# A matrix-memory attention and an expert layer on one core: the hand-written order of 1595 operations replaced by another

## Chip, cores and metric

One core of one Trainium2 chip. The time is device microseconds of one launch of the whole kernel; the number that counts is the median of several runs.

## What is computed

For 4 batches, 8 heads and 768 steps with head size 40, a recurrence with gates (an mLSTM), followed by one expert layer over the 3072 tokens. Cut to what matters:

```python
for t in range(S):
    m_new = np.maximum(f_gate[:, :, t] + m, i_gate[:, :, t])
    f_stab, i_stab = np.exp(f_gate[:, :, t] + m - m_new), np.exp(i_gate[:, :, t] - m_new)
    C = f_stab * C + i_stab * np.einsum('bhd,bhe->bhde', vt, kt)
    n = f_stab * n + i_stab * kt
    y[:, :, t] = sigmoid(o_gate[:, :, t]) * (C @ qt) / max(abs(n @ qt), 1)
...
x = y as (3072 tokens, 320)
h = x @ w_in                                  # 320 -> 2048
g = h * erf(softplus(h))
return g @ w_out                              # 2048 -> 320
```

## The kernel before

The 768 steps are cut into 12 chunks of 64; a chunk of all four batches is 256 tokens. `attention(c)` does a chunk in two halves of two batches each. For each half: scores of k and q on TensorE (PE, L507), times a decay matrix that VectorE applies (DVE, L562), then one accumulation on PE of the carried state (L516), the state's update (L521) and the values under the scores (L530), and on DVE the division, the output gate and the new state (L589 to L616). The half's result is transposed on PE (L389 to L393) and split by ScalarE and VectorE into a high and a low fp32r part, `xh` and `xl` (L402, L406). `gate_block(c)` makes the decays of two chunks at a time: a scan and some ten small operations on DVE, an exponential on ScalarE (ACT), and a round trip through a DRAM scratch `gd` that spreads one row over many partitions (L379, L456, L473).

`mlp(g)` is a quarter of the expert layer for one chunk (48 in all): the up product on PE (L748, two or four operations of 8 to 16 matmuls), copies out of PSUM on ACT (L759) and additions on DVE (L764), softplus and erf on ACT (L768, L772), the product on DVE (L776), a split into high and low fp32r parts `gh` and `gl` (L786 or L788, L792), and the down product on PE (L814 to L817; plain fp32 for the first four, L812). Exp, softplus and erf stand in three different activation tables; each change of table is one ACT_TABLE_LOAD (L876).

The weights arrive as 64-bit numbers. `decode` (L619) rebuilds a float in three operations, two on DVE (L624, L635) and one on ACT (L630); `halves` and `weights_tail` then split it in two (L645 and L649, L683 and L687). All of this happens once, beside the first chunks of attention.

Nothing is scheduled by a compiler. Every operation is recorded by `Plan.add` and has a number; `ORDER` (L94 to L166) lists the 1595 numbers in the order in which they are issued. Each engine works its own instructions off strictly in that order, and SyncE (SP) issues all DMAs in it, on one queue. A negative entry -n issues n warming matmuls at that place (`stay`, L867): matmuls on constants that keep TensorE's clock up and whose results nobody reads. Operation 11 (L279) is five more of them. When an operation needs another activation table than the one loaded, the load goes in just ahead of it (L81), so the number of loads follows from the order.

Names in this text: a00, a01, a10, a11 are the halves of chunks 0 and 1 (chunk, then half; the second half of a chunk comes first in the order); m0, m2, m4 are the first quarters of the expert layer for chunk 0, m47 the last one.

Of the kernel before, what the change touches and what calls it, by code (L numbers as in the profile page):

```python
# [33 lines left out]
class Plan:  # L34
# [60 lines left out]
    1, 4, 0, 3, 5, 7, 9, 11, 12, 6, 13, 2, 14, 15, 16, 8, 17, 33, 27, 32, 34, 36, 35, 20, 19, 31, 38, -1, 40, 28, 26, 29, 93,  # L95
    95, 349, 350, 351, 42, -2, 47, 94, 48, 49, 18, 67, 68, 99, 96, 10, 50, 59, 60, 25, 37, 30, 39, 52, 65, 23, 100, 101, 102,
    105, 107, 106, 108, 41, -2, 55, 44, 66, 72, 56, 109, 43, 24, 71, 354, 45, 46, 111, 112, 57, 74, 76, 58, 22, 69, 73, -1, 64,
    75, 70, 103, 104, 352, 353, 357, 97, 98, 51, 53, 135, 136, 137, 138, 63, 139, 110, 54, 140, 129, 130, 131, 132, 21, 169,
    171, 170, 133, 172, 61, 163, 358, 78, 83, 134, 86, 164, 84, 85, 221, 222, 165, 166, 62, 241, 157, 173, 174, 167, 168, 159,
    239, 240, 125, 127, 158, 160, 175, 199, 200, 161, 242, 88, 193, 77, 91, 201, 195, 205, 207, 223, 224, 225, 162, 273, 79,  # L100
    80, 81, 82, 87, 89, 274, 202, 203, 355, 371, 206, 141, 194, 142, 121, 92, 122, 275, 276, 90, 248, 226, 489, 208, 490, 491,
    204, 196, 249, 227, 356, 369, 113, 209, 250, 143, 197, 251, 361, 114, 372, 210, 115, 494, 149, 126, 128, 492, 457, 467,
    374, 198, 286, 287, 150, 123, 288, 373, 376, 230, 362, 363, 289, 176, 299, 493, 151, 231, 458, 459, 462, 124, 152, 495,
    117, 211, 116, 300, 118, 375, 119, 290, 252, 232, 243, 244, 380, 316, 317, 333, 120, 228, 366, 468, 370, 377, 291, 719,
    720, 378, 382, 212, 359, 364, 365, 721, 185, 384, 360, 496, 253, 145, 379, 392, 337, 233, 245, 389, 186, 724, 466, 368,
    146, 381, 177, 178, 153, 318, 154, 189, 229, 383, 190, 390, 391, 456, 394, 144, 301, 469, 472, 367, 191, 155, 147, 148,
    156, 246, 187, 385, 386, 387, 388, 460, 292, 498, 192, 397, 398, 188, 267, 319, 347, 217, 455, 218, 234, 343, 725, 393,
    395, 396, 268, 461, 474, 320, 277, 302, 235, 247, 181, 497, 399, 400, 278, 464, 475, 473, 236, 477, 465, 470, 334, 182,
    471, 981, 425, 479, 481, 482, 426, 213, 484, 321, 322, 219, 293, 261, 501, 401, 179, 605, 726, 511, 294, 254, 502, 402,
    427, 428, 183, 214, 595, 728, 303, 429, 215, 512, 265, 476, 438, 439, 478, 220, 412, 279, 184, 180, 266, 323, 259, 463,  # L110
    257, 335, 503, 271, 263, 280, 480, 488, 510, 485, 593, 509, 606, 258, 486, 237, 238, 216, 260, 324, 729, 264, 336, 487,
    499, 722, 504, 727, 262, 483, 338, 596, 272, 255, 256, 297, 430, 723, 513, 269, 270, 281, 516, 345, 304, 982, 305, 983,
    505, 295, 298, 500, 296, 325, 339, 340, 326, 327, 597, 440, 506, 431, 508, 986, 413, 306, 307, 329, 330, 414, 331, 519,
    284, 432, 403, 328, 514, 741, 525, 527, 532, 529, 282, 283, 530, 521, 522, 594, 515, 308, 309, 518, 285, 520, 441, 442,
    415, 416, 417, 418, 443, 341, 1243, 603, 523, 344, 524, 742, 312, 313, 310, 404, 405, 348, 526, 550, 551, 406, 576, 990,
    311, 528, 577, 314, 537, 538, 419, 598, 315, 407, 517, 507, 563, 564, 408, 731, 433, 533, 444, 536, 342, 1244, 531, 599,
    608, 740, 552, 553, 554, 607, 539, 540, 565, 732, 534, 535, 1245, 600, 602, 743, 746, 613, 615, 578, 420, 409, 619, 621,
    410, 411, 346, 421, 730, 604, 609, 626, 610, 623, 624, 601, 616, 612, 423, 541, 542, 445, 625, 543, 555, 566, 857, 858,
    859, 614, 617, 618, 611, 620, 424, 436, 579, 631, 632, 633, 640, 641, 642, 733, 736, 622, 634, 635, 630, 636, 652, 653,
    654, 984, 985, 1248, 673, 674, 675, 655, 748, 422, 656, 657, 734, 735, 446, 661, 662, 663, 739, 862, 679, 680, 681, 627,  # L120
    628, 434, 694, 695, 738, 696, 332, 1249, 867, 682, 683, 684, 437, 556, 637, 638, 639, 697, 698, 567, 749, 751, 699, 544,
    700, 701, 755, 658, 659, 660, 580, 664, 702, 545, 629, 451, 452, 453, 744, 745, 987, 703, 676, 435, 677, 678, 685, 752,
    757, 759, 762, 760, 643, 686, 447, 548, 549, 448, 557, 449, 750, 753, 754, 704, 705, 756, 546, 547, 788, 568, 569, 581,
    789, 790, 558, 570, 791, 792, 793, 559, 737, 761, 830, 831, 665, 832, 582, 836, 837, 838, 758, 571, 855, 839, 840, 841,
    687, 561, 809, 815, 562, 574, 988, 989, 810, 816, 811, 644, 450, 767, 868, 869, 872, 768, 817, 860, 861, 856, 766, 666,
    797, 747, 798, 560, 572, 769, 1246, 818, 819, 645, 646, 573, 763, 866, 874, 799, 864, 820, 1247, 764, 765, 873, 776, 777,
    778, 1003, 770, 771, 772, 647, 875, 583, 881, 1004, 1005, 584, 870, 1002, 1119, 575, 794, 795, 773, 774, 796, 775, 667,
    706, 877, 589, 833, 812, 590, 993, 994, 688, 834, 591, 454, 585, 586, 883, 587, 800, 835, 842, 813, 865, 650, 651, 671,
    888, 707, 843, 885, 886, 878, 814, 588, 648, 871, 1129, 1130, 863, 876, 879, 1120, 880, 649, 669, 991, 821, 914, 668, 670,
    690, 779, 689, 915, 916, 882, 708, 1131, 1134, 917, 918, 919, 935, 936, 937, 801, 672, 893, 894, 895, 709, 691, 938, 939,  # L130
    710, 940, 692, 693, 992, 592, 941, 715, 716, 780, 781, 802, 884, 956, 822, 995, 1008, 942, 943, 1010, 962, 887, 892, 957,
    958, 711, 782, 963, 964, 823, 920, 921, 922, 902, 903, 717, 1121, 712, 904, 889, 944, 945, 783, 946, 899, 786, 996, 997,
    900, 901, 1006, 713, 998, 824, 1000, 890, 1001, 896, 1250, 1255, 897, 898, 844, 803, 923, 924, 925, 947, 926, 804, 1128,
    1251, 1011, 825, 1017, 1256, 1007, 965, 966, 959, 960, 961, 891, 784, 1019, 1024, 1021, 1257, 1013, 905, 787, 785, 807,
    808, 1260, 805, 967, 968, 1014, 1022, 948, 1012, 999, 1015, 1016, 828, 1009, 927, 906, 806, 949, 1092, 1093, 1094, 1029,
    845, 829, 1030, 1031, 928, 1095, 1096, 1097, 826, 1018, 950, 951, 1050, 1098, 1020, 1051, 1099, 1052, 1100, 846, 714, 1252,
    1122, 907, 1035, 1036, 1037, 1025, 1026, 1028, 1038, 1039, 1135, 969, 1040, 1118, 1127, 1136, 1117, 1123, 851, 718, 1264,
    1265, 1056, 1124, 1126, 1381, 1057, 1058, 827, 847, 1053, 1054, 1055, 848, 849, 1059, 1060, 1061, 1023, 1101, 1102, 1103,
    929, 852, 970, 1382, 1032, 1125, 1071, 853, 1072, 1073, 1137, 930, 1143, 908, 1033, 1034, 1077, 909, 971, 1078, 1079, 1062,
    1063, 910, 1080, 1139, 1074, 1081, 912, 1027, 1145, 1253, 1147, 1150, 1148, 1140, 1075, 1076, 913, 1132, 1133, 1082, 1268,  # L140
    1254, 933, 934, 911, 954, 1138, 1104, 1105, 1106, 1141, 1142, 1064, 1083, 1041, 1144, 854, 972, 955, 977, 1262, 1149, 1176,
    1177, 1042, 1178, 931, 932, 1218, 1146, 1151, 1219, 1220, 1084, 978, 979, 1263, 980, 1224, 1225, 1226, 1043, 1155, 1156,
    952, 1197, 1157, 1065, 1198, 1152, 1199, 1044, 953, 1185, 1186, 1164, 1154, 1187, 1266, 1267, 1270, 1165, 1166, 973, 1383,
    1045, 974, 975, 1107, 1221, 1222, 1258, 1223, 1161, 1162, 1271, 1048, 1259, 1163, 1390, 1391, 1085, 1269, 1182, 1183, 1200,
    1201, 1184, 1202, 1066, 1153, 1273, 1158, 1159, 1160, 1227, 1228, 1229, 1049, 1275, 1276, 1179, 1180, 1086, 1279, 1181,
    1392, 1395, 1206, 1108, 1069, 1389, 976, 1203, 1167, 1207, 1204, 1070, 1379, 1281, 1286, 1283, 1188, 1189, 1046, 1047,
    1067, 1090, 1208, 1205, 1284, 1272, 1274, 1277, 1068, 1088, 1393, 1380, 1278, 1333, 1334, 1354, 1355, 1087, 1089, 1335,
    1280, 1357, 1358, 1261, 1387, 1356, 1359, 1291, 1292, 1293, 1282, 1287, 1288, 1388, 1360, 1361, 1168, 1362, 1290, 1339,
# [789 lines left out]
```

## Time and profile before

| what | us |
|---|---|
| median of 3 runs | 459.34 |
| lowest and highest run | 458.18, 461.6 |
| span of the profiled execution, first to last instruction | 456.7 |
| TensorE busy in that span | 445.6 (98%) |
| VectorE busy | 336.5 (74%) |
| ScalarE busy | 328.5 (72%) |
| GpSimd busy | 37.3 (8%) |

For the profiled execution the page gives the span alone; what lies around it is the launch and the end of the program, 1.5 us between its span and the lowest run, 2.6 us to the median. How to read it: the busy times say which engine is full on the average, but the first 40 us, the long middle and the last few us have different limits and are read apart. TensorE's busy time includes the warming matmuls.

### The profile page before, as it was taken

The numbers are of one execution on the slowest core, as the hardware profiler recorded it, in microseconds if no ns is written. First come the engines' busy times: TensorE is split into PE (matmuls) and PEld (weight loads), VectorE is DVE, ScalarE is ACT, GpSimd is POOL, SyncE is SP. The second block draws the span as 40 slices with busy tenths as digits, with TensorE's granted clock in tenths as the row PEclk, the third lists the DMA queues.
The fourth block names the chain that finished last, engine by engine and source line by source line (L and its number), as shares of the span: only waits on it lengthen the run. The fifth ranks groups of instructions, "written<-read, shape, count | busy, mean of one in ns | idle before, by whom it ended". The sixth has DMA issues, their size and how long they took to land.

```text
span 456.7 us, 14133 instructions
## 1 busy us (share of the span) xinstructions
PE 445.6 (98%) x6118; PEld 401.6 (88%) x6118; DVE 336.5 (74%) x657; ACT 328.5 (72%) x524; POOL 37.3 (8%) x62
## 2 busy tenths in 40 slices
PE   6979999999999999999999999999999999999996
PEld 4569988888999988989998998899898899999996
DVE  5899989799768766588468948776845869548762
ACT  4758999898976946855996984998445584773760
POOL 2000131003300220001021100001110000000000
PEclk9989999999999999999999999999999999999999
DMA  7889696836613430065405217342341100100011
GB/s 273 273 264 332 170 321 177 217 95 199 184 40 106 136 107 3 3 195 130 133 1 163 72 27 238 72 113 78 107 128 26 30 1 2 29 2 15 1 45 29
DMA packets 46831, 51.82 MB, mean 113 GB/s; under 512 B 27056, under 2 KB 31664, under 8 KB 46768
## 3 DMA queue, kind: packets, MB, share of 16 engines
q1 hardware_dynamic: 46768, 50.91, 38.2%
q8 instruction: 48, 0.79, 0.7%
q14 instruction: 15, 0.12, 0.1%
HBM read 46.77 MB, written 4.13 MB: 111 GB/s over the span
## 4 chain that ended last, share of the span: by engine, by line
PE 92%; DVE 3%; ACT 2%; DMA 1%; issue 1%; SPq 0%; DVEq 0%
PE h L748 40%; PE pob L816 11%; PE pob L814 11%; PE pob L817 11%; PE pa L530 3%; PE pa L507 3%; PE pa L516 3%; PE pa L812 2%; PE pob L812 2%; PE pa L521 2%; PE pa L389 2%; PE pa L444 1%; PE pob L873 1%; DMA eT<-gd 1%; DMA gt<-in_gates_dram 1%
## 5 line engine op out<-in xcount | busy, mean ns | idle before, releaser
L748 PE MATMUL h<-xh,wh 128*128 128x256 f32 (+1 forms) x768 | 201.4, 345 | 0.2 <-DVE hb L764 0.2
L748 PEld LDWEIGHTS h<-xh,wh 128*128 128x128 f32 x768 | 126.0, 190 | 14.1 <-DVE hb L764 0.5
L759 ACT ACTIVATE hb<-h 128x256 f32<-128x256 f32 (+1 forms) x160 | 66.7, 422 | 82.7 <-PE h L748 82.6
L748 PE MATMUL h<-xh,wl 128*128 128x256 f32 x384 | 108.5, 283 | 0.2 <-DVE wl L649 0.2
L816 PE MATMUL pob<-woh,gh 128*128 128x320 f32 x336 | 101.1, 313 | 0.0
L817 PE MATMUL pob<-wo,gh 128*128 128x320 f32 x336 | 100.1, 310 | 0.0
L764 DVE TENSOR_TENSOR hb<-h,hb 128x256 f32<-128x256 f32 x128 | 53.1, 420 | 45.8 <-ACT hb L759 45.2
L748 PEld LDWEIGHTS h<-xh,wl 128*128 128x128 f32 x384 | 72.9, 190 | 2.7 <-DVE wl L649 0.5
L876 ACT ACT_TABLE_LOAD x54 | 69.3, 1283 | 1.7 <-PEq L926 0.8
L776 DVE TENSOR_TENSOR n<-n,hb 128x1024 f32<-128x1024 f32 x48 | 58.6, 1227 | 14.8 <-ACT n L772 14.7
L817 PEld LDWEIGHTS pob<-wo,gh 128*128 128x128 f32 x336 | 63.2, 188 | 1.4
L816 PEld LDWEIGHTS pob<-woh,gh 128*128 128x128 f32 x336 | 63.2, 188 | 0.5
L814 PE MATMUL pob<-woh,gl 128*128 128x320 f32 x336 | 62.7, 312 | 0.0
L485 POOL TENSOR_SCALAR_AFFINE_SELECT dm<-dm 128x512 f32<-128x512 f32 (+1 forms) x40 | 34.0, 856 | 293.9 <-ACT dm L465 256.6
L792 DVE TENSOR_TENSOR gl<-n,gh 128x1024 fp32r<-128x1024 f32 x44 | 53.9, 1228 | 2.2 <-ACT gh L786 1.9
L814 PEld LDWEIGHTS pob<-woh,gl 128*128 128x128 f32 x336 | 53.5, 188 | 2.0
L768 ACT ACTIVATE n<-hb 128x1024 f32<-128x1024 f32 x48 | 49.3, 1058 | 1.6 <-DVE hb L764 1.3
L772 ACT ACTIVATE n<-n 128x1024 f32<-128x1024 f32 x48 | 49.6, 1054 | 0.2
L786 ACT ACTIVATE gh<-n 128x1024 fp32r<-128x1024 f32 x28 | 29.5, 1052 | 0.0
L406 DVE TENSOR_TENSOR xh<-pa,xh 128x384 fp32r<-128x384 f32 x24 | 13.3, 554 | 15.1 <-ACT xh L402 15.1
L562 DVE TENSOR_TENSOR dm<-pa,dm 128x512 f32<-128x512 f32 x24 | 16.5, 687 | 9.6 <-ACT xh L402 6.0
L530 PEld LDWEIGHTS pa<-kvo,dm 64*32 64x32 f32 x1536 | 16.7, 106 | 5.9 <-issue 5.0
(99 smaller groups left out, 469.6 us busy)
## 6 DMA issues: line engine op xcount, KB each, us to landing
qk<-in_qk_dram SPq DMA_DIRECT2D x24, 512.0 KB
kvo<-in_kvo_dram SPq DMA_DIRECT2D x24, 484.0 KB
eT<-gd SPq DMA_DIRECT2D x44, 128.0 KB
raw<-in_w_out_dram SPq DMA_DIRECT2D x16, 320.0 KB
dm<-gd SPq DMA_DIRECT2D x40, 128.0 KB
raw<-in_w_in_dram SPq DMA_DIRECT2D x8, 512.0 KB
out_dram<-o SPq DMA_DIRECT2D x48, 80.0 KB
raw<-in_w_in_dram SPq DMA_DIRECT2D x4, 256.0 KB
```

The source lines that it names most:

```text
L485: nc.gpsimd.affine_select(out=x, in_=x, pattern=[[0, H], [1, L]], compare_op=ALU.is_ge, fill=0.0, base=base, channel_multiplier=-1)
L748: nc.tensor.matmul(h[:, n * T:n * T + n_], w, m, start=(s == 0), stop=(s == len(ops) - 1))
L759: nc.scalar.activation(part(), G(f'h{i}')[:, T:2 * T] if wide else G(f'h{i}'), AF.Copy)
L764: nc.vector.tensor_tensor(part(), G(f'h{i}')[:, 0:T], part(), op=ALU.add)
L768: nc.scalar.activation(new('n0', [128, 1024], ('n0', g)), G('hb'), AF.Softplus)
L772: nc.scalar.activation(G('n0'), G('n0'), AF.Erf)
L776: nc.vector.tensor_tensor(G('n0'), G('n0'), G('hb'), op=ALU.mult)
L792: nc.vector.tensor_tensor(new('gl', [128, 1024], ('gl', g), F32R), G('n0'), G('gh').bitcast(F32), op=ALU.subtract)
L814: nc.tensor.matmul(acc(b), G('gl')[:, ts], woh[:, j], start=False, stop=(j == NFF - 1))
L816: nc.tensor.matmul(acc(b), G('gh')[:, ts], woh[:, j], start=(j == 0), stop=False)
L817: nc.tensor.matmul(acc(b), G('gh')[:, ts], t['wol', j], start=False, stop=False)
L876: plan.run(ORDER, lambda k: nc.scalar.preload_act_table_set(KIND[k]), stay)
```

## The change

`ORDER` is another permutation of the same 1595 operations with the same four warming entries (6 matmuls in all) at other places. No operation, tile, buffer count or DMA is changed. The table has one line more, so all later lines of the changed file are one higher (L748 becomes L749). Of the diff two lines are enough, since its numbers tell a reader nothing:

```diff
 ORDER = [
-    1, 4, 0, 3, 5, 7, 9, 11, 12, 6, 13, 2, 14, 15, 16, 8, 17, 33, 27, 32, 34, 36, 35, 20, 19, 31, 38, -1, 40, 28, 26, 29, 93,
...
+    32, 10, 0, -2, 2, 12, 9, 93, 5, 3, 1, 11, -1, 13, 8, 26, 14, 31, 7, 95, 15, 105, 349, 35, 4, 6, 94, 17, 16, 33, 27, 96,
...
```

The first DMAs that SyncE issues. `cst` are constants, `gt` the gates of two chunks, `kvo` and `qk` the inputs of one half, `raw` a block of encoded weights. Before:

```order
L223 DMA cst<-in_consts_dram 128x12
L293 DMA gt<-in_gates_dram 128x2x128
L439 DMA kvo<-in_kvo_dram 128x968
L435 DMA qk<-in_qk_dram 128x2x512
L439 DMA kvo<-in_kvo_dram 128x968
L657 DMA raw<-in_w_in_dram 128x1024
L293 DMA gt<-in_gates_dram 128x2x128
L657 DMA raw<-in_w_in_dram 128x1024
```

And now:

```order
L440 DMA kvo<-in_kvo_dram 128x968
L224 DMA cst<-in_consts_dram 128x12
L294 DMA gt<-in_gates_dram 128x2x128
L658 DMA raw<-in_w_in_dram 128x1024
L440 DMA kvo<-in_kvo_dram 128x968
L436 DMA qk<-in_qk_dram 128x2x512
L674 DMA raw<-in_w_in_dram 64x1024 x2
L294 DMA gt<-in_gates_dram 128x2x128
```

One `kvo` block went ahead of constants and gates, a weight block went ahead of the second `kvo` and the first `qk`, and the tail block of the weights came up from further down.

TensorE just ahead of the state product of half a10 (`state_71`). Before, three up operations of 16 matmuls had been issued by here, and the transposes of the other half (a11) came right before it:

```order
L748 MATMUL h<-xh,wh 128x256 x2
L389 MATMUL pa<-ident,kvo 128x128 x2
L392 MATMUL pa<-ident,kvo 64x128
L393 MATMUL pa<-ident,kvo 64x128
L516 MATMUL pa<-state_71,qe 64x41 x16
L521 MATMUL pa<-vg,kvo 64x41 x2
```

And now, with four up operations issued by here:

```order
L749 MATMUL h<-xh,wh 128x256 x2
L749 MATMUL h<-xh,wl 128x256
L749 MATMUL h<-xh,wh 128x256 x2
L508 MATMUL pa<-qk 64x64 x16
L517 MATMUL pa<-state_71,qe 64x41 x16
```

One up operation more stands ahead of the heads of a10, and the transposes of a11 went behind them; the scores of a10 (L507, now L508) moved from far ahead to right before them.

ScalarE at the end of the program, from the last copies (L759) on: L768 is softplus, L772 erf, L822 the copy of the output. Before:

```order
L772 ACTIVATE n_6263<-n_6263 128x1024
L759 ACTIVATE hb<-h 128x256
L822 ACTIVATE o<-pob_77 128x320
L822 ACTIVATE o<-pob_76 128x320
L759 ACTIVATE hb<-h 128x256 x2
L772 ACTIVATE n_6220<-n_6220 128x1024
L876 ACT_TABLE_LOAD
L768 ACTIVATE n_6393<-hb 128x1024
L876 ACT_TABLE_LOAD
L772 ACTIVATE n_6393<-n_6393 128x1024
L822 ACTIVATE o<-pob_77 128x320
L822 ACTIVATE o<-pob_76 128x320
```

And now:

```order
L877 ACT_TABLE_LOAD
L769 ACTIVATE n_6303<-hb 128x1024
L877 ACT_TABLE_LOAD
L773 ACTIVATE n_6303<-n_6303 128x1024
L823 ACTIVATE o<-pob_77 128x320
L760 ACTIVATE hb<-h 128x256 x2
L823 ACTIVATE o<-pob_76 128x320
L877 ACT_TABLE_LOAD
L769 ACTIVATE n_6395<-hb 128x1024
L877 ACT_TABLE_LOAD
L773 ACTIVATE n_6395<-n_6395 128x1024
L823 ACTIVATE o<-pob_77 128x320
```

In the piece shown the last two quarters now have a pair of loads each; before, the last one alone had. Over the whole program the loads rise from 54 to 60.

## Rows read from the trace of the kernel before

**Rows 1.** Who waited for whom, TensorE: total us, times, longest.
```profile
PE pob L283 <- DVE state L272: 3.6, 1, 3.6
PE pa L530 <- issue: 1.8, 1, 1.8
PE pa L507 <- issue: 0.9, 2, 0.7
PE h L748 <- DVE wl L649: 0.2, 1, 0.2
```

**Rows 2.** Busy time by stretch (us, instructions), granted clock, DMA share, GB/s.
```profile
0.00:10.00 10.00, 6.28 (x18) 3.96 (x22) 4.75 (x17) 3.96 (x9) 3.34 (x22) 1.00 0.73 255
0.00:33.84 33.84, 27.02 (x510) 17.71 (x510) 25.83 (x66) 20.15 (x49) 3.34 (x22) 0.96 0.85 269
0.00:38.73 38.73, 31.86 (x545) 22.19 (x545) 30.59 (x75) 23.15 (x54) 3.34 (x22) 0.96 0.87 284
50.00:100.00 50.00, 50.00 (x923) 44.75 (x922) 43.85 (x89) 46.84 (x74) 6.14 (x8) 1.00 0.66 186
430.00:445.00 15.00, 15.00 (x100) 14.62 (x99) 10.16 (x12) 9.43 (x12) 0.00 (x0) 1.00 0.15 33
...
30.00:35.00 5.00, 4.77 (x42) 4.42 (x42) 4.69 (x12) 3.01 (x5) 0.00 (x0) 0.66 1.02 312
450.00:457.00 7.00, 2.66 (x19) 2.39 (x17) 0.00 (x0) 0.88 (x2) 0.00 (x0) 1.00 0.21 47
```

**Rows 3.** The chain that ended last: start, us, what; gates, and TensorE at 33.89.
```profile
1.26 2.61 DMA gt<-in_gates_dram
...
33.89 4.22 PE h L748 x30
...
61.93 2.11 PE h L748 x16
```

**Rows 4.** Timeline of the first 12 us: start, us, engine, instruction, idle before.
```profile
2.00 0.59 SPq L439 DMA_DIRECT2D kvo<-in_kvo_dram  x1
...
3.57 4.30 PE L283 MATMUL pob<-state 128*128 128x256 f32 x10 [3.57 <-DVE state L272]
...
3.90 0.48 DVE L303 TENSOR_TENSOR_SCAN m<-gt,m 128x128 f32<-128x128 f32 x1 [0.32 <-DMA gt<-in_gates_dram]
...
8.02 1.96 PE L444 MATMUL pa<-xd,lt 128*128 128x512 f32 x4
...
9.78 0.50 DVE L495 TENSOR_TENSOR vg<-kvo,dm 128x328 f32<-128x328 f32 x1 [1.91 <-ACT dm L449]
...
10.21 2.00 ACT L348 ACTIVATE xd<-x,heads_of 128x64 f32<-128x64 f32 x8
```

**Rows 5.** Timeline of TensorE: the transposes of half a11 and what follows them.
```profile
37.95 0.38 PE L389 MATMUL pa<-ident,kvo 128*128 128x128 f32 x2
...
38.73 0.68 PE L516 MATMUL pa<-state,qe 40*64 40x41 f32 x32
```

**Rows 6.** Costliest groups: the table loads, count | busy us, mean ns | idle before.
```profile
L876 ACT ACT_TABLE_LOAD x54 | 69.3, 1283 | 1.7 <-PEq L926 0.8
```

**Rows 7.** Timeline near the end, 441 to 447 us: ACT, DVE and two L816 groups.
```profile
441.56 1.06 ACT L768 ACTIVATE n<-hb 128x1024 f32<-128x1024 f32 x1 [0.33 <-DVE hb L764]
441.94 0.31 PE L816 MATMUL pob<-woh,gh 128*128 128x320 f32 x1
...
442.65 1.28 ACT L876 ACT_TABLE_LOAD   x1
...
443.69 0.31 PE L816 MATMUL pob<-woh,gh 128*128 128x320 f32 x1
...
443.94 1.06 ACT L772 ACTIVATE n<-n 128x1024 f32<-128x1024 f32 x1
...
445.04 1.23 DVE L776 TENSOR_TENSOR n<-n,hb 128x1024 f32<-128x1024 f32 x1 [1.65 <-ACT n L772]
...
446.30 0.69 DVE L788 CAST gh<-n 128x1024 fp32r<-128x1024 f32 x1
```

141 rows, old and new, of the table ORDER are left out of this document.

## Prediction

> **What bounds the kernel now.** I read the list of who waited for whom first, then busy time by stretch, the chain that ended last, and the timeline of the opening. The list of waits is short [rows 1]: TensorE waits 3.6 us for its first operand, 2.7 us in two places for nothing that the profile shows ("issue"), and the last wait in the opening is 0.2 us for a weight half `wl`, at 33.89 us [rows 1, 3]. From 50 to 100 us TensorE is busy 50.00 of 50.00 us, from 430 to 445 us 15.00 of 15.00 [rows 2]. So behind 34 us the kernel is one queue of matmuls without a hole, and an order can win nothing there; it can only lose. What an order can change is how much of TensorE's real work is done by the time that this queue closes up.
>
> In the opening the engine that sets the pace is VectorE. Up to 33.84 us, the end of the weight half that TensorE waited for, it was busy 25.83 us, so it stood idle for 8.0 us; by 38.73 us it was busy 30.59 us, with 8.1 us idle [rows 2]. Of that idle time 5.25 us fall into the first 10 us (4.75 of 10.00 busy), where it waits for the gates, which land at 1.26 + 2.61 = 3.87 us [rows 3], and then 1.91 us for the exponential of the first decay matrix, until 9.78 us [rows 4].
>
> At the other end the last matmuls run out inside the stretch 450 to 457 us, where TensorE is busy 2.66 us [rows 2]: some 4 us of copy and output DMA follow. The last four operations are the same ones in both orders, so I cost the tail at nothing as long as TensorE gets there without a hole.
>
> **The change part by part.**
>
> *Warming matmuls.* Six before, six after, and the five of L279 stay. Their own cost is unchanged. Two of them now come ahead of L279, on the identity matrix, which GpSimd builds first; so the 3.57 us idle at the start [rows 4] shrinks by about 2 us. That is cover for nothing: the matmuls behind it (L444) still wait for the gates. I count 0.
>
> *VectorE's work ahead of the heads of a10.* The place in the new order with most of VectorE's work ahead of it, measured against TensorE's, is the heads of a10 (L516, state product). When they began in the old order, at 38.73 us, VectorE had done 75 instructions [rows 2, 5]. The new order puts 75 of them ahead too: 3 that are new there (a weight block's L624, L635, L649, together 1.7 us) against 2 fewer (L649 and L687, 1.4 us), with durations of the same kind of instruction; so 30.59 + 0.3 = 30.9 us of VectorE work. TensorE has one up operation more behind it by then: 16 matmuls, about 2.0 us (2.11 us with a state product before it [rows 3]), and three transposes fewer (38.73 - 37.95 = 0.78 us [rows 5]). Net, 1.2 us more of TensorE's work is behind it. So if VectorE loses as much idle time as before (8.0 us), the heads of a10 start at 38.9 instead of 38.73 us with 1.2 us more done: a gain of 1.2 - 0.2 = 1.0 us, which the closed queue carries to the end.
>
> *VectorE's idle time in the new opening.* Three things move it.
> First, one `kvo` block of 484 KB goes ahead of constants and gates. The gates come later by the issue alone, 0.59 us, at the least, and by that plus its whole transfer at the most. The opening's mean is 255 GB/s [rows 2], so 1.9 us and 2.5 us in all. Transfers that are all on one queue went one behind the other so far, but at the very start the DMA engines are empty; I take 1.3 us, gates at 5.1 us.
> Second, from the gates to L444 the chain is the same, 8.02 - 3.90 = 4.1 us [rows 4], plus about 0.5 us for a weight decode (L624) and `heads_of`, which now stand inside it: L444 starts at about 9.7 us, 1.7 us later.
> Third, on ScalarE the eight small copies of L348, 2.00 us [rows 4], now stand before the exponential that L495 waits for; they were behind it. The exponential can start when the copies end. Before, L495 followed L444 by 9.78 - 8.02 = 1.8 us; with this it is some 2.2 us, so 11.9 us instead of 9.78.
> Against this, VectorE has decode work of the first weight block to do while it waits (1.0 us), the first half's L495 and L562 no longer alternate with holes, and behind 12 us its row of work has more raw weights landed early, since the tail block and the next ones are issued sooner; I find only small holes (0.2 to 0.3 us at four places, where it waits for TensorE or ScalarE by turns). Sum: 4.3 us until the gates, 1.6 us for the exponential, 0.4 us for the first scores, about 1.0 us of small holes, some 0.6 us between instructions: 7.9 us. The low end is 5.5 us (everything behind the gates hidden but the exponential), the high end 8.0 + 2.2 + 1.5 = 11.7 us (nothing of the later start made up, and one late scratch round trip `gd`). I take 7.9 us: no change against 8.0.
>
> *TensorE's clock.* After the hole of 1.8 us before 30 us the granted clock in 30 to 35 us is 0.66 [rows 1, 2], between its levels of 1.2 and 2.4 GHz. A stretch at the lower level loses 0.34 of 5 us, 1.7 us. In the new order I find holes of about 1.8 us before L444 and 1.4 us before the heads of a00, so such a drop may come earlier, in front of small matmuls, where TensorE is ahead of VectorE and the loss is covered. Where it hits the up operations between 27 and 38 us, the cover is the 1.4 us for which they would else wait at a10. I count 0, with 1.7 us kept for the high end.
>
> *Six more table loads.* Each is 1283 ns [rows 6]: 7.7 us on ScalarE, which is idle 3.2 us of 50 from 50 to 100 us, and 5.6 us of 15 at 430 to 445 us [rows 2]. By the two orders some 11 to 13 of them lie in the first 100 us of TensorE's work in both; in the last 40 us there are nine instead of four, 6.4 us more. The last pair is on the chain to the last quarter: load 1.28, softplus 1.06, load 1.28, erf 1.06, product 1.23, cast 0.69 [rows 7], 6.6 us. TensorE has six pairs of down products between m47's last up operation and the first matmul that needs it, 443.69 - 441.94 = 1.75 us each [rows 7], 10.5 us. That leaves 3.9 us for the copies and additions before the softplus: hidden, 0 us.
>
> After the load at 442.65 us the erf starts at 443.94 us, so the load costs its own 1.28 us and nothing else [rows 7]. The Trainium skill (ScalarE: Activation LUTs, "What ACT_TABLE_LOAD costs") says that each switch also drains the engine, about 1.38 us more, 2.66 us in all. By that the chain would be 2.8 us longer, 9.4 us, and 1.1 us would be left for the copies; six loads would be 16 us of ScalarE. The row shows no drain, so the sum goes by the row.
>
> *The long middle.* At 50 to 100 us VectorE is busy 43.85 and ScalarE 46.84 of 50 us, and TensorE still had no hole [rows 2]. The new order has VectorE's work there no further ahead. I count 0, and up to 3 us for holes from a late scratch load or a late slot.
>
> **Sum.** 456.7 - 1.0 = 455.7 us of span. The median stands 2.6 us above the profiled span; with the same distance the median is 458.3 us. That is 0.2%, which a measurement of this kernel can't tell from no change: about 1% is what it can.
>
> **The rivals.**
> *Faster, VectorE really packed (chance 0.12).* The idle time falls to its low end, 5.5 us: 2.4 us more. If TensorE's clock also keeps its upper level throughout, the 1.7 us of half clock are gone where the queue closes: 459.3 - 1.0 - 2.4 - 1.7 = 454.2 us. For it: more weights are fetched early, and the up operations begin some 4 us sooner. Against it: the gates come later.
> *Slower, the gates behind `kvo` (chance 0.15).* The late gates and the copies of L348 before the exponential move the whole opening of attention by 2.2 us, and VectorE makes none of it up, because the next weights wait on SP behind `gd`, whose issue needs a later exponential. The idle time is 11.7 us: 3.7 us more, and a stretch at half clock costs 1.7 us uncovered: 459.3 - 1.0 + 3.7 + 1.7 = 463.7 us. It decides from a first L495 later than 12 us on. For it speaks the order on SP and ScalarE; against it that VectorE has raw weights to decode meanwhile.
> *Loads at the end (chance 0.05, within the forecast's own range).* If TensorE's last pairs don't cover ScalarE, since copies take more than the 3.9 us that are left, the end costs about 1.7 us: 460 us. It would be decided by copies and additions over 3.9 us, where the output's copy stands among them too [rows 7].
>
> **How the numbers follow.** Forecast, no change that can be told: 0.73 (the case of the loads in it), with 458.3 us and its own range of 455.5 to 462. The rivals hold the rest; the range is 454.4 to 462.8 us. Faster by over 1% (under 454.7): 0.12; within 1%: 0.73; slower (over 463.9 at the median's 1%): 0.15, since the middle can add to the slower case.
>
> **What would show it.** Right: TensorE without waits behind 39 us, at the latest; VectorE idle about 8 us in the first 39 us; gates landing at 5 us, the first L495 (now L496) at about 12 us; the first up operation at 26 to 27 us instead of 30.26; one wait of TensorE, 1 to 1.5 us, before the heads of a10; 60 loads without a wait at the end. Wrong: TensorE waits behind 50 us that sum to over 2 us, or a first up operation later than 30 us.

## The result, and the profile after

| | median, us | lowest to highest | runs |
|---|---|---|---|
| before | 460.33 | 458.1 to 461.9 | 6 |
| after | 464.97 | 461.92 to 468.66 | 6 |

The ratio is 1.0112, with a 95% interval of 1.0069 to 1.0156: slower, by 4.6 us at the median. That is about 1%: little, but clear of the noise. The profiled execution of after took 463.12 us, with a span of 461.4 us; 4.7 us more than the span of before (456.7), so the two traces hold the loss.

TensorE is the bound as before, and who waited for whom is the first view to read, as in [rows 1]. After, the list of TensorE's waits begins so (total us, times, longest):

```profile
PE pa L517 <- DVE qe L479: 2.7, 3, 1.3
PE pa L445 <- ACT lt L341: 2.1, 1, 2.1
PE pob L874 <- POOL ident masks.py:199: 1.4, 1, 1.4
PE pa L531 <- issue: 1.4, 1, 1.4
PE pa L818 <- DVE wo L714: 1.1, 1, 1.1
PE pa L445 <- ACT state L588: 0.9, 1, 0.9
PE h L749 <- DVE xh L407: 0.7, 1, 0.7
PE pa L522 <- DVE vg L496: 0.6, 1, 0.6
```

Before, the waits behind the start were "issue" and twice 0.2 us for VectorE. Now six of the eight rows shown end at a hand-over from VectorE or ScalarE. The busy time by stretch says where, with columns as in [rows 2] (TensorE, its weight loads, VectorE, ScalarE and GpSimd busy; then granted clock, DMA share, GB/s):

```profile
0.00:10.00 10.00, 6.70 (x16) 3.59 (x16) 4.81 (x18) 4.00 (x9) 3.31 (x22) 1.00 0.78 242
0.00:33.84 33.84, 26.59 (x493) 17.21 (x493) 23.33 (x61) 20.00 (x46) 3.31 (x22) 1.00 0.80 240
0.00:38.73 38.73, 31.31 (x556) 21.65 (x556) 27.43 (x70) 24.31 (x54) 3.31 (x22) 1.00 0.84 242
50.00:100.00 50.00, 49.77 (x869) 45.23 (x869) 42.23 (x94) 44.17 (x73) 8.60 (x8) 1.00 0.72 210
...
40.00:45.00 5.00, 4.22 (x132) 3.17 (x125) 4.63 (x12) 4.59 (x7) 0.00 (x0) 0.74 1.00 350
100.00:150.00 50.00, 47.34 (x744) 42.61 (x743) 41.44 (x81) 42.19 (x60) 5.35 (x8) 1.00 0.55 164
430.00:445.00 15.00, 15.00 (x99) 14.46 (x98) 9.55 (x14) 12.56 (x15) 0.00 (x0) 1.00 0.06 13
```

Two places lose. In the opening VectorE has done 27.43 us of work by 38.73 us instead of 30.59, so it stood idle for 11.3 us instead of 8.1; TensorE was busy for 40.81 us of the first 50 instead of 43.13, 2.3 us less. And from 100 to 150 us TensorE is idle for 2.7 us. At the end, 430 to 445 us, it is full again.

Why VectorE stands idle in the opening, its own timeline says: `DVE qe` is the product of the queries with the decays `eT`, which come back from the DRAM scratch `gd`.

```profile
31.14 0.69 DVE L479 TENSOR_TENSOR qe<-qk,eT 104x512 f32<-104x512 f32 x1 [1.95 <-issue]
...
33.35 0.43 DVE L625 TENSOR_SCALAR raw<-raw 128x512 int32<-128x512 int32 x1 [0.31 <-DMA raw<-in_w_in_dram]
...
35.43 0.43 DVE L625 TENSOR_SCALAR raw<-raw 128x512 int32<-128x512 int32 x1 [0.20 <-DMA raw<-in_w_in_dram]
...
38.88 0.69 DVE L479 TENSOR_TENSOR qe<-qk,eT 104x512 f32<-104x512 f32 x1 [0.61 <-DMA eT<-gd]
```

The wait named "issue" is one for `eT` too: it ends 0.07 us after the last part of that DMA had landed, at 31.07 us; 15 of its 16 parts were there by 29.69 us. With the two waits for weight blocks that were issued behind the read-back, these four come to 3.1 us, about what VectorE stands idle more.

The DMAs that SyncE issued (start, us, what) show how that round trip became late:

```profile
13.23 0.35 SPq L380 DMA_DIRECT2D gd<-x  x1
13.62 0.37 SPq L658 DMA_DIRECT2D raw<-in_w_in_dram  x1
14.04 0.33 SPq L380 DMA_DIRECT2D gd<-x  x1
14.41 0.34 SPq L440 DMA_DIRECT2D kvo<-in_kvo_dram  x1
14.80 0.43 SPq L658 DMA_DIRECT2D raw<-in_w_in_dram  x1
15.27 0.43 SPq L436 DMA_DIRECT2D qk<-in_qk_dram  x1
15.75 0.96 SPq L658 DMA_DIRECT2D raw<-in_w_in_dram  x2
16.75 0.91 SPq L380 DMA_DIRECT2D gd<-x  x2
25.57 1.30 SPq L474 DMA_DIRECT2D eT<-gd  x2
```

Two of the four `gd` writes, 8 KB each, were issued at 16.75 us behind five loads of 2.5 MB together. In the DMA records their packets moved only from 23.41 to 24.84 us, as those loads ended; the read-back was issued at 25.57 us, at 17.94 us before. From 17.66 to 25.57 us SyncE issued nothing, so the weight blocks behind the read-back came late with it. The next read-back, of a10, was issued at 30.30 us instead of 27.73. TensorE's timeline has the consequence at the heads of a11 and a10:

```profile
31.98 0.68 PE L517 MATMUL pa<-state,qe 40*64 40x41 f32 x32 [1.26 <-DVE qe L479]
39.72 0.68 PE L517 MATMUL pa<-state,qe 40*64 40x41 f32 x32 [1.16 <-DVE qe L479]
41.04 0.66 PE L522 MATMUL pa<-vg,kvo 64*64 64x41 f32 x32 [0.65 <-DVE vg L496]
```

Behind these three holes the granted clock falls: 0.74 in 40 to 45 us, where transposes and up products stand that nothing covers. Before had such a stretch too, 0.66 in 30 to 35 us [rows 2]; over the first 50 us the mean granted clock is 0.97 in both kernels.

In the middle, the timeline from 107.95 us on shows a gate block (L313 to L319) on VectorE ahead of the weight split L714 that a down product (L818) waits for, and GpSimd's `affine_select` (L486) beside it:

```profile
107.95 0.28 DVE L313 TENSOR_TENSOR x<-gt,m 128x128 f32<-128x128 f32 x1
108.22 1.38 POOL L486 TENSOR_SCALAR_AFFINE_SELECT dm<-dm 128x512 f32<-128x512 f32 x2 [17.30 <-ACT dm L466]
108.27 0.74 DVE L314 TENSOR_TENSOR x<-x,m 128x128 f32<-128x128 f32 x1
109.05 0.82 DVE L316 TENSOR_TENSOR_SCAN x<-keep,x 128x128 f32<-128x128 f32 x1
...
110.57 1.34 DVE L714 TENSOR_TENSOR wo<-wo,woh 128x320 fp32r<-128x320 f32 x2
...
111.96 0.41 PE L818 MATMUL pa<-wo,gh 128*128 128x320 f32 x1 [1.11 <-DVE wo L714]
```

The wait of 1.35 us (1.4 in the list) that is given as "issue" is one of this kind too: it stands ahead of all 64 matmuls of the heads, the product `dm` (L563) ends at 129.00 + 0.68 us, and TensorE goes on 0.10 us later.

```profile
129.00 0.68 DVE L563 TENSOR_TENSOR dm<-pa,dm 128x512 f32<-128x512 f32 x1
...
129.78 0.81 PE L531 MATMUL pa<-kvo,dm 64*32 64x41 f32 x64 [1.35 <-issue]
```

To place the loss, each matmul was given the usual time of its shape, and the moments were compared at which equal amounts of such work were done in the two traces. The work stands in another order, so this is rough: after is some 2 us earlier at 12 us of work, 2.1 to 2.5 us later from 25 to 60 us of work, about 6 us later at 105 us, and 4.7 us later at 400.

### The profile page after: what moved, and what is told of

Read it like the earlier page. It is cut to its first block, busy times and chain, and to the rows that moved or that the text cites. A ratio compares the mean times of both kernels' runs of the same rounds, so it can differ in the third digit from the quotient of the medians.

```text
span 461.4 us, 14142 instructions
## 1 busy us (share of the span) xinstructions
PE 445.3 (97%) x6118; PEld 400.6 (87%) x6118; DVE 337.4 (73%) x657; ACT 338.1 (73%) x530; POOL 36.2 (8%) x62
## 4 chain that ended last, share of the span: by engine, by line
PE 79%; DMA 7%; DVE 6%; ACT 3%; SPq 2%; issue 2%; DVEq 0%; ACTq 0%
PE h L749 35%; PE pob L817 11%; PE pob L815 11%; PE pob L818 11%; PE pa L531 3%; DMA eT<-gd 2%; PE pa L517 2%; PE pa L508 2%; DMA gd<-x 2%; PE pa L390 1%; DMA raw<-in_w_out_dram 1%; PE pa L522 1%; DVE n L777 1%; DMA gt<-in_gates_dram 1%; DMA raw<-in_w_in_dram 1%
## 5 line engine op out<-in xcount | busy, mean ns | idle before, releaser
L749 PE MATMUL h<-xh,wh 128*128 128x256 f32 (+1 forms) x768 | 202.8, 344 | 0.7 <-DVE xh L407 0.7
L749 PEld LDWEIGHTS h<-xh,wh 128*128 128x128 f32 x768 | 126.2, 189 | 14.7 <-DVE xh L407 0.9
L749 PE MATMUL h<-xh,wl 128*128 128x256 f32 x384 | 108.0, 281 | 0.0
L818 PE MATMUL pob<-wo,gh 128*128 128x320 f32 x336 | 99.9, 309 | 0.0
L877 ACT ACT_TABLE_LOAD x60 | 77.0, 1283 | 1.8 <-PEq L927 0.8
L749 PEld LDWEIGHTS h<-xh,wl 128*128 128x128 f32 x384 | 72.6, 189 | 1.9
L818 PEld LDWEIGHTS pob<-wo,gh 128*128 128x128 f32 x336 | 63.1, 188 | 1.7
L486 POOL TENSOR_SCALAR_AFFINE_SELECT dm<-dm 128x512 f32<-128x512 f32 (+1 forms) x40 | 32.9, 828 | 303.2 <-ACT dm L466 301.8
L479 DVE TENSOR_TENSOR qe<-qk,eT 104x512 f32<-104x512 f32 x22 | 16.0, 726 | 8.7 <-DMA eT<-gd 6.7
```

The source lines that it names most:

```text
L486: nc.gpsimd.affine_select(out=x, in_=x, pattern=[[0, H], [1, L]], compare_op=ALU.is_ge, fill=0.0, base=base, channel_multiplier=-1)
L749: nc.tensor.matmul(h[:, n * T:n * T + n_], w, m, start=(s == 0), stop=(s == len(ops) - 1))
L818: nc.tensor.matmul(acc(b), G('gh')[:, ts], t['wol', j], start=False, stop=False)
L877: plan.run(ORDER, lambda k: nc.scalar.preload_act_table_set(KIND[k]), stay)
```

## The experiments

Theory: the late scratch round trip makes the opening's loss, gate blocks put early on VectorE the middle's. Rivals: the late gates of the forecast's slower case; and, as the runs went on, TensorE's wait for its own code. All runs are compared with runs of before on the same chip; edits are edits of the table `ORDER` unless told otherwise.

| kernel | median, us | ratio to before [95%] |
|---|---|---|
| h1, new opening, old rest | 462.79 | 1.0065 [1.0042, 1.0087] |
| h2, old opening, new rest | 460.80 | 1.0023 [1.0000, 1.0046] |
| g1, scratch early in after | 462.85 | 1.0063 [1.0037, 1.0088] |
| m1, gate blocks later in after | 464.03 | 1.0094 [1.0062, 1.0127] |
| g1m1, both | 463.11 | 1.0081 [1.0055, 1.0107] |
| k1, g1 and gates first | 463.98 | 1.0090 [1.0063, 1.0118] |
| h1g1, g1's opening, old rest | 461.93 | 1.0044 [1.0022, 1.0066] |
| t1, scratch late in before | 462.31 | 1.0069 [1.0045, 1.0094] |
| m2, gate blocks sooner in before | 464.02 | 1.0105 [1.0077, 1.0132] |
| b1, loads sooner in before | 459.02 | 1.0003 [0.9980, 1.0026] |
| f1, g1 with its code shifted | 466.04 | 1.0135 [1.0108, 1.0162] |
| f2, before with its code shifted | 468.25 | 1.0193 [1.0164, 1.0222] |
| bf, b1 and f2 | 469.40 | 1.0215 [1.0183, 1.0248] |
| g3, g1 with a load later | 463.21 | 1.0086 [1.0051, 1.0121] |
| hg3, g3's opening, old rest | 462.01 | 1.0057 [1.0034, 1.0080] |

**Which part of the order loses: h1 and h2.**

```diff
-ORDER = OLD
+ORDER = NEW[:186] + [x for x in OLD if x not in NEW[:186]]   # h1
+ORDER = OLD[:188] + [x for x in NEW if x not in OLD[:188]]   # h2
```

> The first 186 entries of the new order, then what is left in the old order; the same up operations have been issued at the seam. Theory A (the opening loses at the scratch round trip gd to eT, which stands behind 2.5 MB of loads; the middle loses at two hand-overs on VectorE): the opening's loss alone is left, 2.4 us by TensorE's lag at 28 us of its work (the changed kernel against before), so 1.005 of before; TensorE waits at 32 and 39 us as in the changed kernel and has none behind 60 us. Rival B (the late gates and ScalarE's copies L348 cost the opening): the same time, but for another reason. Rival C (the six more table loads cost the time): this kernel has the old rest and 54 loads or so, so no more than 1.001.

> The first 188 entries of the old order, then what is left in the new order. Theory A: the opening is that of before, the waits of 1.1 us (down product for a weight half, 112 us in the changed kernel) and 1.4 us (heads of a40, 130 us) stay, so 2.5 to 3.5 us over before: 1.006, and no wait behind 150 us. Rival C (table loads): the loss grows behind 400 us, where nine loads stand instead of four, and the whole 4.7 us stay: 1.010. If the losses need the new opening's lateness to show, 1.000.

The opening alone gives 1.0065, the rest alone 1.0023; their product, 1.0088, lies inside the interval of the whole change. About three quarters of what they give is the opening's. A part of h1's is the seam's: TensorE waits 1.7 us for `hb` at 53 and 57 us there, which neither order does.

Both traces miss a part of what was expected. h1 has no wait of TensorE for `qe` at 32 and 39 us: its read-back was issued as late as in after, at 25.03 us, but `qe` began at 29.95 us. VectorE then waited 2.41 us for a weight block behind the read-back, and TensorE 1.90 us for `wh` at 35.46 us; m1, below, has the same wait (2.27 and 1.27 us). So the late round trip shows at one or the other of the two. h2 stands far under the 1.006 expected: of the two waits in the middle it has the second alone (1.39 us at 128.06 us), and one of 1.53 us for `qe` at 89.17 us. The two traces of the result divide TensorE's idle time about evenly between the opening (2.3 us) and the middle (2.7 us), so three quarters is a rough share.

**The scratch write, undone in after (g1) and put into before (t1).**

```diff
-60, 23, 37, 111, 68, 66
+60, 23, 21, 24, 37, 111, 68, 66
...
-103, 129, 21, 71
+103, 129, 71
...
-137, 53, 24, 69
+137, 53, 69
```

> The changed kernel with two of the four scratch writes gd of the first gate block (L379, operations 24 and 21) issued right behind the first two instead of behind five loads of 2.5 MB. Theory A: eT for a11 lands at 27.5 to 28.5 us instead of 30.04, VectorE's wait of 1.95 us and TensorE's of 1.26 us go, the loads behind it start about 8 us sooner, eT for a10 is there in time, and the half clock at 42 to 46 us goes too: 2.5 to 3.8 us less than the changed kernel, so 1.002 to 1.005 of before. Rival B (late gates, L348 ahead of the exponential): these are untouched, so within 0.5 us of the changed kernel, 1.010. Rival C: 1.010.

```diff
-109, 43, 24, 71
+109, 43, 71
...
-58, 22, 69
+58, 135, 129, 24, 22, 69
```

> The old order, with one scratch write (op 24) put behind the inputs of a10 and two 512 KB weight loads that came later, as in the new order; its read-back (eT of a11) follows. Theory: eT of a11 lands some 4 us later, at 27 to 28 us instead of 23.4, VectorE waits 2 to 3 us for it, the heads of a11 follow late, and the median rises by 1.5 to 3 us (461.5 to 462.5 if before stands at 460). Rival (VectorE decodes the weights that land earlier meanwhile and makes it up): within 0.5 us of before.

t1 cost 2.4 us, the size that the theory had. Its read-back was issued at 23.73 us, and TensorE's list of waits has the wait for `qe`, but a larger one beside it:

```profile
PE pa L530 <- issue: 3.6, 1, 3.6
PE pa L507 <- issue: 2.2, 2, 1.9
PE pa L516 <- DVE qe L478: 1.2, 1, 1.2
```

The late write does cost (b1, below, has the same two loads sooner without it and loses nothing), but mostly by another way than the theory's: of the 4.3 us that TensorE waits more than in before, 1.2 us are for `qe` and 3.1 us in holes named "issue".

g1 took the waits for `qe` out of the opening, and in its timeline too a hole inside L530 stood there instead:

```profile
31.95 0.65 PE L530 MATMUL pa<-kvo,dm 64*32 64x41 f32 x47
...
35.10 0.37 PE L530 MATMUL pa<-kvo,dm 64*32 64x41 f32 x17 [2.50 <-issue]
```

So g1 gave back 0.5% of the 1.1%, not all of it, and the two intervals overlap. Its profiled execution was its shortest (459.89 us), 3 us under its median; what the others lost there no profile shows.

**The late gates: k1.**

```diff
-32, 10, 0, -2, 2, 12
+0, 12, 32, 10, -2, 2
...
-96, 19, 34, 28, 20
+96, 34, 28, 19, 20
```

> g1 with constants and gates ahead of the first kvo block on SyncE, and the two exponentials of the first decay matrices ahead of the eight copies of L348 on ScalarE: the two places on which the slower rival of the prediction rests. If that rival's terms (gates late, exponential behind the copies) cost time at the end, this is 1 to 2 us faster than g1 and g1m1 (461 us or less). If they are made up by 12 us of TensorE's work, as the comparison of the two traces has it, the first L495 comes 2 us sooner and the median is that of g1 within 0.7 us (462 to 463).

The first L495 moved from 12.81 us in g1 to 10.88 us, and the median was no better than g1's (1.0090 against 1.0063, the intervals overlap). So earlier gates bring no gain that can be seen, and the late ones are not shown to cost anything at the end.

**The opening with the old rest: h1g1.** The edit of g1, cut and joined as in h1.

> The opening of the new order with its two late scratch writes put right behind the second one, and the old order for all that follows. Theory (the opening's loss is the scratch round trip that waits behind 2.5 MB of loads): no wait of TensorE for qe (L516) in the first 45 us, and some 2 us less than h1_new_opening (462.8), so 460 to 461 us, ratio to before about 1.001. Rival (the loss is VectorE's late start behind the late gates, and the scratch only one sign of it): another wait of like size takes its place, 462 to 463 us, ratio 1.005 or more.

No wait for `qe` is left, and the ratio fell from 1.0065 to 1.0044 (the intervals overlap), less than half of what the theory wanted, with a hole of 2.27 us inside L530; 0.9 us of the seam's waits for `hb` stand in it too. The rival is right in that another wait takes the place.

**What the hole is: f1 and f2.** A hole in the middle of one operation can't be a wait for an operand that another engine makes, since this kernel waits for those ahead of the operation's first matmul. (The holes that VectorE ended, as at 129.78 us in after, do stand there.) The trace holds another kind of packet: 48 of 16 KB on a queue of their own, called instruction. TensorE ran 6118 matmuls and 6118 weight loads, 255 to a packet. In all profiled runs there are 28 holes over 0.5 us named "issue" that VectorE did not end, and each ends 1.23 to 1.76 us after the last such packet did. Before has two of them (0.70 and 1.83 us), after none. To test it, 32 tiny matmuls shift the code behind them, by 128 instructions in f1 (on g1, with all five warming matmuls kept) and by 120 in f2 (on before, with two warming matmuls fewer):

```diff
-        for _ in range(5):
+        for _ in range(3):
             nc.tensor.matmul(pob[1][:, 0:256], zeros[:, 0:128], zeros[:, 0:256], start=True, stop=True)
+        for _ in range(32):
+            nc.tensor.matmul(pob[1][0:32, 0:32], zeros[0:64, 0:32], zeros[0:64, 0:32], start=True, stop=True)
```

> g1 with 32 tiny warming matmuls (64 by 32) more at the start, where TensorE waits 1.7 us anyway. They write nothing that is read; what they move is the place of the code's refills, by 64 matmuls and 64 weight loads. Theory (code): g1's hole of 2.50 us inside L530 of a11 leaves its place: it shrinks below 1 us or goes, since the refill is then asked for among up operations some 2 us sooner; 460 to 461.5 us if nothing else takes its place. Rival (operand): a hole of over 2 us after the 47th matmul of the same L530, 462 to 463.

> The old order with the same 32 tiny matmuls in place of two of the five warming matmuls of L279. Theory (code): the hole of 1.83 us inside L530 leaves its place, since the third refill is asked for some 2 us sooner, when few loads are queued; with the half clock behind it 1.5 to 3.5 us less, 456.5 to 458.5. Rival (operand): the hole stays behind the 46th matmul of L530, and the median is that of before within 0.7 us.

The holes left their places, so code it is; the gain that I expected didn't come. f1 has its holes at 24.10, 44.61 and 98.22 us and a median 1.0135 of before. In f2's list, where L509, L532 are the scores and heads and L875 a warming matmul, the hole at 29.95 us is gone and others came, at 43.13, 73.86 and 130.41 us among them:

```profile
PE pa L532 <- issue: 3.0, 4, 1.5
PE pa L509 <- issue: 2.5, 1, 2.5
PE pob L875 <- issue: 1.4, 1, 1.4
```

f2's span is 7.7 us over that of before: 6.2 us more in waits of TensorE over 0.1 us (3.7 us of it in code holes), and 1.5 us more busy. 120 instructions that do nothing cost 9 us at the median, twice what the change cost. Any other order of TensorE's work moves these places too, so the small differences between the versions here can hold a part of this kind; no run takes it out.

**How long the code takes: b1, bf.** b1 issues two weight loads 3 us sooner, at a time when SyncE was idle.

```diff
-58, 22, 69, 73
+58, 22, 69, 135, 129, 73
```

> The old order with two 512 KB weight loads (ops 135, 129) issued right behind the read-back eT of a11, some 3 us sooner, instead of at 22.5 us. Theory (the hole inside L530 at 29.95 us is TensorE waiting for its code, whose refill is asked for at about 22.5 us and lies behind bulk loads): the refill's packet comes at 25 to 26 us instead of 27.63, the hole shrinks from 1.83 to under 1 us, with it the stretch at half clock, and the median falls by 1 to 3 us (457 to 459). Rival (the hole is a wait for an operand): hole and median as before, within 0.7 us.

> The old order with both edits, loads sooner (b1) and code shifted (f2): the version meant to beat both kernels. Theory (code): no hole over 0.7 us between 25 and 45 us, no stretch at half clock before the end, 455.5 to 458 us. Rival (operand, or another wait behind it): no better than before, 459 to 461.

b1's timeline has the smaller hole, and a new wait four microseconds on:

```profile
29.09 0.38 PE L530 MATMUL pa<-kvo,dm 64*32 64x41 f32 x18 [0.83 <-issue]
...
33.91 0.39 PE L748 MATMUL h<-xh,wl 128*128 128x256 f32 x1 [1.00 <-DVE wl L649]
```

The hole fell from 1.83 to 0.83 us and no stretch at half clock was left before the end, as expected; TensorE then reached VectorE's weight half `wl` sooner and waited 1.00 us for it instead of 0.23, and the median stayed (1.0003). So in before the hole and the half clock stood in time in which TensorE would else have waited for the weights. bf, meant to have none, has seven code holes (1.70 us at 29.97 and 1.09 us at 42.09 us among them). For the third packet of code, worked out from the DMA records (asked for: when TensorE began its instruction 652, the place that fits the 48 packets of before best; no record shows the asking itself), in us:

```
kernel  asked for  packet moved     TensorE stops  goes on  hole
before  22.5       27.63 to 28.58   28.12          29.95    1.83
b1      22.6       26.37 to 27.65   28.26          29.09    0.83
t1      22.5       31.21 to 32.62   30.47          34.05    3.58
g1      25.3       32.53 to 33.72   32.60          35.10    2.50
g3      26.3       32.20 to 33.70   33.64          35.20    1.56
after   25.1       28.27 to 29.24   (waits for qe)          none
```

In the middle many packets come 1.0 to 1.4 us after that place; this third one took 3.2 to 8.7 us in all the kernels here. Queued loads alone don't explain it: from 25 to 27 us in after the DMA engines were busy for 1% of the time, from 23 to 25 us in t1 for 14% and from 22 to 24 us in f2 for 8%, and the packet came at 28.27, 31.21 and 26.82 us. So either it is asked for later than the fit has it, or something else holds it up: that stays open. What g1 did can be read off without the fit: in after the packet had come by 29.24 us, before TensorE's wait for `qe` began at 30.72 us; in g1, whose loads run on through that time, it came 4.3 us later, and TensorE ran out of code.

**Less bulk ahead of the code: g3 and hg3.** The load of `qk` for a10 goes behind the `kvo` of a10.

```diff
-164, 57, 222
+164, 222
...
-86, 58, 239
+86, 58, 57, 239
```

> g1 with the 512 KB load of qk for a10 (op 57), issued at 24.1 us, put behind the kvo of a10, so that less is queued when TensorE asks for its third refill of code at 25.3 us. Theory: the refill comes 1.5 to 2 us sooner than in g1 (7.2 us after it was asked for), the hole of 2.5 us inside L530 shrinks to 0.5 to 1 us, median 1 to 2 us under g1 (461 to 462 with before at 459.7). Rival (the hole does not depend on loads, or the scores of a10 now wait for qk): 462.5 to 464.

> The same opening as g3, with the old order behind it. Theory (scratch and code refill are all that the new opening loses): 459 to 460.5 us, ratio 0.999 to 1.002. Rival (a third loss in the opening): that of h1g1, 1.004 or more.

In g3 the code came 5.9 us after it was asked for (7.2 in g1) and the hole shrank to 1.56 us, but not the median. In hg3 it came 6.8 us after that place, as in h1g1 (6.7), and nothing changed. The theory's direction is seen in one of two, its gain in neither: what keeps the new opening behind the old once the scratch is early is not settled beyond the hole itself and the seam's 0.7 to 0.9 us.

**The middle: m1, g1m1, m2.** Op 983 belongs to the gate block of chunk 8, op 1245 to that of chunk 10.

```diff
-593, 983, 265, 441, 344, 238, 258, 322
+593, 265, 441, 344, 238, 258, 983, 322
...
-517, 1245, 986
+517, 986
...
-403, 525, 284
+403, 525, 1245, 284
```

> The changed kernel with VectorE's parts of two gate blocks (chunks 8 and 10, some five operations each) moved back by a few places: the first behind the weight split that a down product waits for, the second behind the scores' product that the heads of a40 wait for. Theory A: TensorE's waits of 1.1 us at 112 us and 1.4 us at 130 us go, 2.0 to 2.6 us less than the changed kernel, 1.005 to 1.007 of before. Rival C (table loads, spread over the program): no change, 1.010. If VectorE is simply full there, the wait moves to the next hand-over and the time stays.

> The new order with both earlier edits: scratch writes early (g1) and two gate blocks later on VectorE (m1). If the losses of the opening and of the middle add up, the ratio is the product of what the two gave, 1.0112 - 0.005 - 0.002, about 1.004 (461.6 us with before at 460). Rival: the middle's waits only move on to the next hand-over, whatever stands ahead, and the ratio is that of g1 alone, 1.006.

The waits at 111.96 and 129.78 us went; others came, 1.2 us for `qe` at 90.6, 1.0 us for `gl` at 117.6 and 0.6 us at 133.7. Neither run gained what it should: 1.0094, and 1.0081 for both edits. m2 puts the blocks of chunks 8 and 10 early into the old order, at the same hand-overs:

```diff
-606, 258, 486
+606, 982, 983, 258, 486
...
-741, 525, 527
+741, 1243, 1244, 1245, 525, 527
```

> The old order with the gate blocks of chunks 8 and 10 put early on VectorE, ahead of the weight split that the down product waits for (op 258) and ahead of the scores' product of a40 (op 525), as in the new order. Theory (these blocks are what the middle loses): TensorE waits of 1 us or more for VectorE at 105 to 130 us, 1 to 2.5 us more than before. Rival (VectorE in the old order is far enough ahead there, and the new order's middle is late as a whole because the opening was late): waits under 0.5 us in sum, within 0.7 us of before.

It cost 4.9 us at the median. In its timeline both waits of the middle stand right behind a moved block; the second ends 0.10 us after VectorE's `dm`:

```profile
106.50 0.60 PE L360 MATMUL pa<-ident,x 128*128 128x32 f32 x4 [1.64 <-DVE kvo L601]
...
127.18 0.51 PE L530 MATMUL pa<-kvo,dm 64*32 64x41 f32 x33 [1.53 <-issue]
```

Both waits stand ahead of their operation's first matmul (the second row is cut off by its window). So moving the gate blocks ahead of hand-overs costs 3.2 us of waits with an opening that is not late, but not by the blocks' work alone: VectorE's scan in the second block (L303, 124.10 us) had itself waited 1.91 us for its gates, whose load SyncE had issued at 121.20 us. That m1 did not win its waits back says that VectorE is late there for more than these two blocks.

No version beat before; b1 equals it.

## Why the prediction was wrong, step by step

- *Warming matmuls, table loads, tail*: right. TensorE is busy 15.00 of 15.00 us at 430 to 445 us beside the additional loads, ScalarE 12.56 instead of 9.43. The row of the loads is in the page with the same 1283 ns as in [rows 6], 60 of them:

```profile
L877 ACT ACT_TABLE_LOAD x60 | 77.0, 1283 | 1.8 <-PEq L927 0.8
```

 A load at 446.11 us is followed by the erf at 447.40, again without the drain of some 1.38 us that the Trainium skill (ScalarE: Activation LUTs, "What ACT_TABLE_LOAD costs") has.
- *The gain of 1.0 us at a10*: the fourth up operation did stand ahead of its heads, but these began at 39.72 us, 0.8 us later than the forecast's 38.9, met a second hole of 0.65 us and had the half clock behind them: the gain was lost there.
- *VectorE's idle time in the opening, 7.9 us*: the first of two steps that failed, with 11.3 us measured. Gates and first L496 were near the forecast (12.56 us for 11.9), the first up operation at 25.33 us for 26 to 27. The error is in what was set against the late start: the weights "issued sooner" were entered as work for VectorE only, and not as 2.5 MB ahead of two `gd` writes on the same queue. The text had "one late scratch round trip" in the high end alone; it was the case. A second error hid half of it: the 75 instructions (30.9 us) "ahead" of a10 were all that VectorE had done by then. In before the `qe` that a10 needs ended at 37.24 us, behind 29.2 us of work; in after it ended at 39.57 us, behind 28.1 us. With 30.9 us ahead and the idle time measured, a10 would have begun some 3 us later still.
- *TensorE's clock, 0 us*: right as a sum, not as an argument. Both kernels have a stretch near half clock, and the mean over the first 50 us is the same, 0.97. But the forecast had the new one covered; it fell behind three holes (0.74 in 40 to 45 us) in front of up operations, while the old one was the covered one, as b1 shows. What the uncovered one costs no run shows by itself.
- *The long middle, 0 us*: the other step that failed, with 2.7 us of TensorE's time lost from 100 to 150 us. The rule used, that VectorE's work stands no further ahead, looked at sums over a stretch. The two waits there, 2.5 us, each stand behind a gate block on VectorE, of 2.7 us and 3.2 us here. That the blocks are the whole cause is not shown: m1 moved them, these waits went, and others came.
- *The holes named "issue"* [rows 1] were taken as a given of the kernel. They are code refills, whose length depends on the order: 0.83 to 3.58 us at the same place.
- *The slower rival* (463.7 us, idle 11.7) had the size and its sign (first L495 later than 12 us), but not the mechanism: k1 put the gates first, had its first L495 1.9 us sooner and won nothing. Scratch and weights did wait for each other, but the other way round first: the scratch behind loads, and only then the next loads behind the scratch, as the rival had it. That its size came near is luck.

## What to carry to other kernels

On one DMA queue, count the bytes issued ahead of every small transfer that something waits for: here two 8 KB writes, issued at 16.75 us behind 2.5 MB, moved from 23.41 us on, and their read-back and the loads behind it waited for them; so such writes belong ahead of loads that have time. Price a moved block on an engine by the next hand-over behind it, not by how busy the engine is on the average. And when an edit moves loads, look at the packets of TensorE's code as well: in g1 the third one came 4.3 us later than in after, and a hole of 2.50 us took the place of the waits that the edit had removed.

## What the runs showed of the hardware

- TensorE can stop in the middle of an operation for its code: 28 holes of 0.5 to 3.6 us, each ended 1.23 to 1.76 us after a 16 KB packet. They fall into the dense small matmuls of attention or right behind them (25 inside, one in transposes, two in warming matmuls), where some 250 instructions pass in 2 to 5 us, and none of them into the up and down products.
- The third packet of code came 3.2 to 8.7 us after the place that fits as its request; elsewhere 1.0 to 1.4 us were often enough. The Trainium skill (DMA: Bandwidth & Descriptors, "Queues, rings and completion order") says that each DMA engine takes turns between its queues, packet by packet. By that alone a packet on its own queue would not have to wait until another queue's loads are through. No run here decides it: g1 looks otherwise (7.2 us among loads), but in t1 the packet took 8.7 us though the DMA engines stood nearly idle for 2 of them (14% busy), and the time of asking is a fit.
- VectorE's operations took longer beside GpSimd's `affine_select`: 0.74 us at 108.27 us for an operation that took 0.29 us in before, and 0.82 us for the scan beside it that took 0.42 us in before; beside the next `affine_select` (122.31 to 125.02 us) the operations of L313 and L314 took 1.24 and 0.69 us, 0.28 and 0.29 us in before.
